# First batch of a fused attention and feed-forward kernel: numerators ahead of the inverse, kept in SBUF, and three weight transfers behind a new gate

## The chip, the cores and the metric

The kernel runs on one core of one Trainium2 chip. The metric is the device time of a whole execution in microseconds. Four executions of the kernel before took 314.83 to 316.83 us, with a median of 316.32 us.

## The reference, cut to what matters

Linear attention with cosine and sine weights, and a feed-forward layer behind it. There are 8 batches of 8 heads, 576 positions and a head size of 64. The feed-forward layer goes from 512 to 2048 and back to 512, over 8 x 576 = 4608 tokens.

```python
q_p = phi(q, cos_w, sin_w)      # relu(q) times cos and sin, side by side: 128 features
k_p = phi(k, cos_w, sin_w)
kv = einsum('bhsf,bhsd->bhfd', k_p, v)
z = sum(k_p, axis=2)
num = einsum('bhsf,bhfd->bhsd', q_p, kv)
den = einsum('bhsf,bhf->bhs', q_p, z) + 1e-06
x = num / den                   # then tokens by 512
h = x @ w_in
out = (h * sigmoid(1.702 * h)) @ w_out
```

## The kernel before

**Order.** Every engine runs its instructions in the order in which they stand in the program; the order is written out by hand, with no scheduler behind it. A prologue prepares the attention of batch 0 alone. Then a loop `i` over nine blocks of 512 tokens runs the feed-forward layer: `mm1(i, n)` for the 16 column groups `fc` of `w_in` (four matmuls and a gelu each, steps n = 0 to 15), and `mm2` for the output (64 matmuls, steps 16 to 31). Between these steps, as entries `at(n, ...)`, stands the attention of batch `i + 1`. In block 0 they start at step 6: `prep_q` (step 6, relu of q), `transpose_pe` (steps 8 to 11: TensorE transposes, then VectorE's product `qT` with cos and sin), `prep_v` (steps 8 to 12: ten VectorE products `vt`), `prep_k` (steps 13 and 14: relu of k into `kr`), `unit_kv(1)` at step 15, and `unit_den`, `unit_spread` and `unit_num` behind it.

**One batch of attention.** `unit_kv` makes the sums over positions, k times v, in two PSUM tiles, copies the sums of k into `zbuf` (L294) and the rest into `kvs` (L300). `unit_den` (L310, L314) makes the denominators; VectorE inverts them (L320), and L325 and L326 turn the inverse into `comb`. `unit_spread` (L338) spreads `comb` with 16 matmuls per batch over the 64 rows of each head, and ScalarE copies the result into SBUF as `invb` (L343). `unit_num` (L356) makes the numerators, 16 matmuls for each half `hf` of the positions, and VectorE multiplies them with `invb` into `xT` (L359), which is the input of `mm1`. A batch has four pairs of heads `j` and two halves `hf`, so eight tiles of 128 x 288.

**PSUM.** There are eight banks: four under the name `at`, two `hps`, two `yps`, each name a ring. `warmup(n)` is n matmuls whose result nobody reads.

**Transfers and their gates.** SP's queue loads q, v and k; each batch has a main part (512 positions) and a tail (64). POOL's queue loads the weights, each in four groups of 512 KB, with a change of type from float32. Two kinds of gate order them: a one-element POOL copy that reads what must have landed (L455 for `w_in`, L466 for `w_out`), and a one-element transfer on SP that reads a group of weights (L458 reads the second group of `w_in`, and batch 1's loads stand behind it; L469 reads the third group of `w_out`, and batch 2's loads stand behind it). The first four column groups of block 0 are computed outside the loop (`first`), with the contraction chunk `kc` as the outer loop.

Of the kernel before, what the change touches and what calls it, by code (L numbers as in the profile page):

```python
# [12 lines left out]
F32 = mybir.dt.float32  # L13
# [3 lines left out]
MUL = mybir.AluOpType.mult  # L17
# [11 lines left out]
def kernel(  # L29
# [9 lines left out]
    nc = tc.nc  # L39
    B, H, S, D = q.shape  # L40
    d_model = H * D
    d_ff = moe_w_in.shape[1]
    NP = H // 2
# [3 lines left out]
    HF = S // 2  # L47
    NSEG = 4
    SEG = S // NSEG
# [4 lines left out]
    two = ctx.enter_context(tc.tile_pool(name="two", bufs=2))  # L54
# [8 lines left out]
    def hps_tile():  # L63
        return ps.tile([128, TB], F32, name="hps", bufs=2)

    def yps_tile():
        return ps.tile([128, TB], F32, name="yps", bufs=2)

    def at_tile():
        return ps.tile([128, TB], F32, name="at", bufs=4)  # L70

    def warmup(n):
        for _ in range(n):
            wps = hps_tile()
            nc.tensor.matmul(wps, warm[:, 0:128], warm, start=True, stop=True)  # L75

    state = {b: {} for b in range(B)}
# [6 lines left out]
    def load_tail(t, src, b, on):  # L84
        on.dma_start(  # L85
            out=t[0:64, 2048:2560].rearrange("p (h d) -> p h d", h=H),
            in_=src[b, :, 512:576, :].rearrange("h p d -> p h d"))
# [117 lines left out]
    xT = one.tile([128, NP, B * S], BF16)  # L205
# [74 lines left out]
    def unit_kv(b):  # L280

        s = state[b]
        kv4 = [at_tile()[:, 0:2 * VW].rearrange("p (j e) -> p j e", j=2) for _ in range(2)]
        for j in range(NP):
            for c in range(5):
                for hh in range(2):
                    w = 64 * (hh ^ (j % 2))
                    nc.tensor.matmul(kv4[j // 2][w:w + 64, j % 2], kr[:, c, j, 64 * hh:64 * hh + 64],  # L288
                                     vt[:, c, 2 * j + hh, :], start=(c == 0), stop=(c == 4))
        s["kvs"], s["zs"] = [], zbuf[b % 2]  # L290
        for n, kv in enumerate(kv4):
            for hh in range(2):
                r = slice(64 * hh, 64 * hh + 64)
                nc.vector.tensor_copy(s["zs"][r, 2 * n:2 * n + 2, :, ds(12 + 16 * hh, 4)],  # L294
                                      kv[r, :, 128:130].unsqueeze(3).to_broadcast([64, 2, 2, 4]))
        for kv in kv4:
            kvs = two.tile([128, 2, 2, D], BF16, name="kvs", bufs=4)
            kv5 = kv[:, :, 0:128].rearrange("p j (cs e) -> p j cs e", cs=2)
            if b == 0:
                nc.scalar.copy(kvs, kv5)  # L300
            else:
                nc.vector.tensor_copy(kvs, kv5)
            s["kvs"] += [kvs[:, jj] for jj in range(2)]

    def unit_den(b):

        s = state[b]
        den_ps = at_tile()
        if b == 0:
            nc.tensor.matmul(den_ps[:, 0:SEG], ones[0:3, :], epsm[0:3, :], start=True, stop=False)  # L310
        for g in range(NSEG):
            for cs in range(2):
                for j in range(NP):
                    nc.tensor.matmul(den_ps[32 * j:32 * j + 32, 0:SEG], s["zs"][:, j, cs, ds(12 - 4 * g, 32)],  # L314
                                     s["qT"][:, j, cs, ds(g * SEG, SEG)],
                                     start=(b > 0 and g == 0 and cs == 0), stop=(g == NSEG - 1 and cs == 1))
        inv, pa, pb, comb = [two.tile([128, SEG], dt, name=f"den{n}", bufs=1)
                             for n, dt in enumerate((F32, F32, F32, BF16))]
        if b == 0:
            nc.vector.reciprocal(inv, den_ps[:, 0:SEG])  # L320
        else:
            nc.vector.tensor_scalar(pa, den_ps[:, 0:SEG], 1e-6, None, op0=ADD)
            nc.vector.reciprocal(inv, pa)
        for o, m in ((pa, 0), (pb, 1)):
            nc.vector.tensor_tensor(o.bitcast(I32), inv.bitcast(I32), bits[:, m:m + 1].to_broadcast([128, SEG]), op=AND)  # L325
        nc.vector.tensor_tensor(comb, pa, pb, op=SUB)  # L326
        s["comb"] = comb
        s["invb"] = {}

    def unit_spread(b, hf):  # L330
        s = state[b]
        if b == 0 and hf == 1:
            bps = [hps_tile(), hps_tile(), yps_tile(), yps_tile()]
        else:
            bps = [at_tile() for _ in range(NP)]
        for g2 in range(2):
            for j in range(NP):
                nc.tensor.matmul(bps[j][:, ds(g2 * SEG, SEG)],  # L338
                                 sel[32 * j:32 * j + 32, 2 * hf + g2].rearrange("p hh d -> p (hh d)"),
                                 s["comb"][32 * j:32 * j + 32, :], start=True, stop=True)  # L340
        for j in range(NP):
            invb = two.tile([128, HF], F32, name="invb", bufs=8)
            nc.scalar.copy(invb, bps[j][:, 0:HF])  # L343
            s["invb"][j, hf] = invb

    def unit_num(b, hf, j2s=(0, 1)):

        s = state[b]
        num_ps = {j: at_tile() for j2 in j2s for j in (2 * j2, 2 * j2 + 1)}
        for j2 in j2s:  # L350
            for cs in range(2):
                for jj in range(2):
                    j = 2 * j2 + jj
                    for hh in range(2):
                        r, w = 64 * (hh ^ jj), 64 * hh
                        nc.tensor.matmul(num_ps[j][w:w + 64, 0:HF], s["kvs"][j][r:r + 64, cs, :],  # L356
                                         s["qT"][r:r + 64, j, cs, ds(hf * HF, HF)], start=(cs == 0), stop=(cs == 1))
        for j, t in num_ps.items():
            nc.vector.tensor_tensor(xT[:, j, ds(b * S + hf * HF, HF)], t[:, 0:HF], s["invb"][j, hf], op=MUL)  # L359


    gT = {}
# [1 line left out]
    def mm1_part(hps, i, fc, kc):  # L364
        nc.tensor.matmul(hps, w_in_sb[:, kc, ds(fc * 128, 128)], xT[:, kc, ds(i * TB, TB)],  # L365
                         start=(kc == 0), stop=(kc == NP - 1))
# [69 lines left out]
    junk = const.tile([1, 16], F32)  # L436
# [23 lines left out]
    for name, src in SRC:  # L460
# [2 lines left out]
        load_part(state[1][name], src, 1, 0, H)  # L463
        if name != "kf":
            load_tail(state[1][name], src, 1, nc.sync)
    nc.gpsimd.tensor_copy(junk[:, 1:2], state[1]["vf"][0:1, 0:1])  # L466
    for g in range(4):
        nc.gpsimd.dma_start(out=w_out_sb[:, ts(g, 4), :], in_=wout_r[:, ts(g, 4), :])
    nc.sync.dma_start(out=junk[:, 9:10], in_=w_out_sb[0:1, 8, 0:2].bitcast(F32))  # L469
    load_all(2)  # L470
    warmup(14)
    unit_kv(0)
    warmup(4)
    unit_den(0)
    warmup(8)
    for hf in range(2):
        unit_spread(0, hf)
    for j2 in range(2):
        for hf in range(2):
            unit_num(0, hf, (j2,))  # L480
    first = [hps_tile(), hps_tile(), yps_tile(), yps_tile()]
    for kc in range(NP):
        for fc in range(4):
            mm1_part(first[fc], 0, fc, kc)
    for fc in range(4):
        gelu(first[fc], fc)

# [1 line left out]
    for i in range(NBLK):  # L489
        work = {n: [] for n in range(40)}  # L490
        b = i + 1
# [4 lines left out]
        if b < B:  # L496
            k0 = 6 if i == 0 else 0
            at(k0, prep_new, b)
            at(k0, prep_q, b, 0)
            at(k0, prep_q, b, 1)  # L500
            if i == 0:
                for j in range(NP):
                    at(k0 + 2 + j, transpose_pe, b, j, 0)
                    at(k0 + 2 + j, transpose_pe, b, j, 1)
            else:
                at(k0, transpose_dma, b)
                if b + 1 < B:
                    at(k0 + 1, load_all, b + 1)
            for c in range(5):
                for cs in range(2):  # L510
                    at(k0 + 2 + c, prep_v, b, c, cs)
            at(k0 + 7, prep_k, b, 0, 4)
            at(k0 + 7, prep_k_tail, b)
            at(k0 + 8, prep_k, b, 4, 8)
            if i > 0:
                for j in range(NP):
                    at(k0 + 9 + j, prep_trig, b, j)
            k1 = 15 if i == 0 else 12
            at(k1, unit_kv, b)
            at(k1 + 3, unit_den, b)  # L520
            for hf in range(2):
                at(k1 + 7 + 6 * hf, unit_spread, b, hf)
                at(k1 + 10 + 6 * hf, unit_num, b, hf)
# [49 lines left out]
```

## Time and profile before

| | |
|---|---|
| time, median of 4 (lowest to highest) | 316.32 us (314.83 to 316.83) |
| the profiled execution: time, span | 314.83 us, 312.9 us |
| PE busy | 303.3 us, 97% |
| DVE busy | 135.5 us, 43% |
| ACT busy | 135.4 us, 43% |
| POOL busy | 46.7 us, 15% |
| granted TensorE clock | 1.0 |

The span runs from the first to the last instruction of the profiled execution; 314.83 - 312.9 = 1.93 us of its time lie around the span. PE is TensorE's matmuls, PEld its weight loads, DVE VectorE, ACT ScalarE, POOL GpSimd, SP the engine that only issues transfers. In an answer of the timeline the first column is the start in us from the span's start, the second the time, and the brackets at the end tell the idle time ahead of the group and what ended it. In the chain of waits each row is a start, a duration and what held the end back in that time; the chain is followed from the last instruction backwards.

### The profile page before, as it was taken

The numbers are of one execution on the slowest core, as the hardware profiler recorded it, in microseconds if no ns is written. First come the engines' busy times: TensorE is split into PE (matmuls) and PEld (weight loads), VectorE is DVE, ScalarE is ACT, GpSimd is POOL, SyncE is SP. The second block draws the span as 40 slices with busy tenths as digits, with TensorE's granted clock in tenths as the row PEclk, the third lists the DMA queues.
The fourth block names the chain that finished last, engine by engine and source line by source line (L and its number), as shares of the span: only waits on it lengthen the run. The fifth ranks groups of instructions, "written<-read, shape, count | busy, mean of one in ns | idle before, by whom it ended". The sixth has DMA issues, their size and how long they took to land.

```text
span 312.9 us, 5644 instructions
## 1 busy us (share of the span) xinstructions
PE 303.3 (97%) x2216; PEld 139.4 (45%) x2216; DVE 135.5 (43%) x344; ACT 135.4 (43%) x260; POOL 46.7 (15%) x106
## 2 busy tenths in 40 slices
PE   8799989999999999999999999999999999999994
PEld 3444544345444544454444444544444444444443
DVE  4853863487255634654375348523952210000000
ACT  5644511463336433652365236533554346226511
POOL 7800400210220011000210120002101200011021
PEclk9999999999999999999999999999999999999999
DMA  7999999958926971596259824881500220011022
GB/s 216 272 206 312 236 197 293 236 137 257 240 67 112 330 159 67 119 326 156 67 109 289 203 68 103 279 216 52 109 18 9 60 67 0 36 67 35 2 67 67
DMA packets 60110, 45.85 MB, mean 147 GB/s; under 512 B 28916, under 2 KB 57844, under 8 KB 60084
## 3 DMA queue, kind: packets, MB, share of 16 engines
q1 hardware_dynamic: 51012, 31.60, 38.8%
q0 software_dynamic: 7328, 13.37, 19.1%
q10 hardware_dynamic: 1744, 0.52, 0.8%
q8 instruction: 17, 0.28, 0.4%
q14 instruction: 9, 0.07, 0.1%
HBM read 36.70 MB, written 9.44 MB: 147 GB/s over the span
## 4 chain that ended last, share of the span: by engine, by line
PE 85%; DMA 9%; DVE 3%; SPq 1%; POOL 0%; issue 0%; DVEq 0%
PE yps L401 38%; PE hps L365 36%; DMA vf<-in_v_dram 7%; PE at L356 3%; PE at L288 3%; DMA w_in_sb<-in_moe_w_in_dram 2%; PE hps L401 2%; DVE vt L277 1%; PE at L314 1%; PE yps L425 1%; PE at L338 1%; DVE qT L244 1%; DVE kr L217 0%; POOL w_in_sb L457 0%; SPq L80 0%; SPq L85 0%
## 5 line engine op out<-in xcount | busy, mean ns | idle before, releaser
L365 PE MATMUL hps<-xT,w_in_sb 128*128 128x512 bf16 x568 | 129.1, 378 | 0.6 <-DVE xT L359 0.4
L401 PE MATMUL yps<-w_out_sb,g 128*128 128x512 bf16 x528 | 120.5, 380 | 0.0
L370 ACT ACTIVATE g<-hps 128x512 bf16<-128x512 f32 x142 | 84.7, 597 | 55.9 <-PE hps L365 55.8
L365 PEld LDWEIGHTS <-w_in_sb 128*128 128x128 bf16 x576 | 54.8, 97 | 70.2 <-issue 10.2
L401 PEld LDWEIGHTS <-g 128*128 128x128 bf16 x560 | 51.9, 98 | 63.3 <-issue 2.9
L413 POOL DMA_DIRECT2D out_dram<-ysb x54 | 30.6, 569 | 239.4 <-ACT invb L343 129.7
L411 ACT COPY ysb<-yps 128x512 f32<-128x512 f32 x31 | 18.1, 585 | 82.7 <-PE yps L401 63.5
L359 DVE TENSOR_TENSOR xT<-at,invb 128x288 bf16<-128x288 f32 x64 | 24.7, 449 | 66.7 <-PE at L356 66.7
L343 ACT COPY invb<-at 128x288 f32<-128x288 f32 x60 | 19.7, 419 | 20.2 <-PE at L338 20.2
L430 DVE COPY ysb<-yps 128x256 f32<-128x256 f32 x1 | 0.4, 425 | 57.2 <-PE yps L425 57.2
L256 DVE TENSOR_TENSOR qT<-qTr,trig 128x1152 bf16<-128x1152 bf16 x24 | 16.6, 753 | 16.8 <-DMA qTr<-qn 14.3
L277 DVE TENSOR_SCALAR vt<-vf,cosw 128x512 bf16<-128x512 f32 (+1 forms) x40 | 18.9, 480 | 0.5 <-DMA vf<-in_v_dram 0.5
L217 DVE TENSOR_SCALAR qn<-qf 128x512 bf16<-128x512 f32 (+2 forms) x52 | 14.3, 339 | 7.0 <-DMA qf<-in_q_dram 6.8
L277 DVE TENSOR_SCALAR vt<-vf,sinw 128x512 bf16<-128x512 f32 (+1 forms) x36 | 17.3, 480 | 0.0
L75 PE MATMUL hps<-warm 128*128 128x512 bf16 x47 | 13.2, 439 | 1.2 <-DVE halfpi L121 1.2
L288 PE MATMUL at<-vt,kr 128*64 128x130 bf16 x320 | 10.9, 221 | 2.5 <-ACT kr L215 1.5
L356 PE MATMUL at<-qT,kvs 64*64 64x288 bf16 x256 | 12.2, 289 | 0.4 <-ACT invb L343 0.3
L217 DVE TENSOR_SCALAR kr<-kf 128x1024 bf16<-128x1024 f32 (+1 forms) x23 | 12.5, 591 | 0.0
L288 PEld LDWEIGHTS <-kr 128*64 128x64 bf16 x320 | 9.3, 109 | 6.2 <-issue 2.5
L356 PEld LDWEIGHTS <-kvs 64*64 64x64 bf16 x256 | 6.4, 105 | 8.0 <-issue 7.7
L75 PEld LDWEIGHTS <-warm 128*128 128x128 bf16 x47 | 4.8, 109 | 7.9 <-issue 3.2
L294 DVE CAST zbuf<-at 64x16 bf16<-64x16 f32 x32 | 5.5, 172 | 5.7 <-PE at L288 5.0
(75 smaller groups left out, 106.0 us busy)
## 6 DMA issues: line engine op xcount, KB each, us to landing
qf<-in_q_dram SPq DMA_DIRECT2D x8, 1024.0 KB, 6.1
vf<-in_v_dram SPq DMA_DIRECT2D x8, 1024.0 KB, 8.9
kf<-in_k_dram SPq DMA_DIRECT2D x7, 1024.0 KB, 11.7
out_dram<-ysb POOLq DMA_DIRECT2D x38, 128.0 KB, 2.5
out_dram<-ysb POOLq DMA_DIRECT2D x16, 256.0 KB, 2.7
w_in_sb<-in_moe_w_in_dram POOLq DMA_DIRECT2D x4, 512.0 KB, 8.5
w_out_sb<-in_moe_w_out_dram POOLq DMA_DIRECT2D x4, 512.0 KB, 9.7
kf<-in_k_dram SPq DMA_DIRECT2D x2, 512.0 KB, 11.1
```

Of the source, the lines that this page charges most:

```text
L75: nc.tensor.matmul(wps, warm[:, 0:128], warm, start=True, stop=True)
L217: on.tensor_scalar(o, i, 0.0, None, op0=MAX)
L277: on.tensor_scalar(o, i, w, None, op0=MUL)
L288: nc.tensor.matmul(kv4[j // 2][w:w + 64, j % 2], kr[:, c, j, 64 * hh:64 * hh + 64], vt[:, c, 2 * j + hh, :], start=(c == 0), stop=(c == 4))
L343: nc.scalar.copy(invb, bps[j][:, 0:HF])
L356: nc.tensor.matmul(num_ps[j][w:w + 64, 0:HF], s["kvs"][j][r:r + 64, cs, :], s["qT"][r:r + 64, j, cs, ds(hf * HF, HF)], start=(cs == 0), st ...
L359: nc.vector.tensor_tensor(xT[:, j, ds(b * S + hf * HF, HF)], t[:, 0:HF], s["invb"][j, hf], op=MUL)
L365: nc.tensor.matmul(hps, w_in_sb[:, kc, ds(fc * 128, 128)], xT[:, kc, ds(i * TB, TB)], start=(kc == 0), stop=(kc == NP - 1))
L370: nc.scalar.activation(g, hps, AF.Gelu_apprx_sigmoid)
L401: nc.tensor.matmul(yps, gT[fc][:, ds(t * 128, 128)], w_out_sb[:, fc, :], start=(fc == 0), stop=(fc == FC - 1))
L411: nc.scalar.copy(ysb, cur[t])
L413: nc.gpsimd.dma_start(out=out[row:row + (n - 1) * step + 1:step, :], in_=ysb[p0:p0 + n, :])
```

## The change

For batch 0 the numerators are made right after the denominators' matmuls, ahead of the inverse: the first half into two `hps` and two `yps` tiles, the second into four `at` tiles. ScalarE copies the eight numerator tiles into SBUF (where it copied the eight spread tiles before). Then `comb` is spread into PSUM and VectorE multiplies the spread tiles, straight from their banks, with the numerators in SBUF. The eight warmup matmuls ahead of the spread go. Half of batch 0's copies into `zbuf`, two of four, move from VectorE to ScalarE, where they stand ahead of the two `kvs` copies. The four first column groups of `mm1` run in pairs: `kc` 0 and 1 for `fc` 0 and 1, then for `fc` 2 and 3, then `kc` 2 and 3 in the same way. On POOL, the first group of `w_out` stays gated on v of batch 1, and the last three groups get a second gate, on k of batch 1. Batches 1 to 7 keep their order on every engine.

```diff
@@ unit_kv
-                nc.vector.tensor_copy(s["zs"][r, 2 * n:2 * n + 2, :, ds(12 + 16 * hh, 4)],
-                                      kv[r, :, 128:130].unsqueeze(3).to_broadcast([64, 2, 2, 4]))
+                o = s["zs"][r, 2 * n:2 * n + 2, :, ds(12 + 16 * hh, 4)]
+                i = kv[r, :, 128:130].unsqueeze(3).to_broadcast([64, 2, 2, 4])
+                if b == 0 and hh == 1:
+                    nc.scalar.copy(o, i)
+                else:
+                    nc.vector.tensor_copy(o, i)
@@ new functions: spread and num hold the matmuls of L338 and L356
+    def to_sbuf(b, hf, tiles):
+        for j in range(NP):
+            t = two.tile([128, HF], F32, name="invb", bufs=8)
+            nc.scalar.copy(t, tiles[j][:, 0:HF])
+            state[b]["sb", j, hf] = t
+
+    def product(b, hf, tiles, js=range(4)):
+        for j in js:
+            nc.vector.tensor_tensor(xT[:, j, ds(b * S + hf * HF, HF)], tiles[j][:, 0:HF], state[b]["sb", j, hf], op=MUL)
@@ the weights
-    nc.gpsimd.tensor_copy(junk[:, 1:2], state[1]["vf"][0:1, 0:1])
     for g in range(4):
+        if g < 2:
+            nc.gpsimd.tensor_copy(junk[:, 1 + g:2 + g], state[1][("vf", "kf")[g]][0:1, 0:1])
         nc.gpsimd.dma_start(out=w_out_sb[:, ts(g, 4), :], in_=wout_r[:, ts(g, 4), :])
@@ the prologue
     unit_den(0)
-    warmup(8)
     for hf in range(2):
-        unit_spread(0, hf)
-    for j2 in range(2):
+        tiles = [at_tile() for _ in range(NP)] if hf else [hps_tile(), hps_tile(), yps_tile(), yps_tile()]
+        num(0, hf, tiles)
+        to_sbuf(0, hf, tiles)
+    tiles = [[hps_tile(), hps_tile(), yps_tile(), yps_tile()], [at_tile() for _ in range(NP)]]
+    for hf in range(2):
+        spread(0, hf, tiles[hf])
+    for js in ((0, 1), (2, 3)):
         for hf in range(2):
-            unit_num(0, hf, (j2,))
+            product(0, hf, tiles[hf], js)
     first = [hps_tile(), hps_tile(), yps_tile(), yps_tile()]
-    for kc in range(NP):
-        for fc in range(4):
-            mm1_part(first[fc], 0, fc, kc)
+    for kcs, fcs in (((0, 1), (0, 1)), ((0, 1), (2, 3)), ((2, 3), (0, 1)), ((2, 3), (2, 3))):
+        for kc in kcs:
+            for fc in fcs:
+                mm1_part(first[fc], 0, fc, kc)
```

More of the change, by code (lines that the diff above doesn't have):

```diff
@@ L327, in unit_den, with spread, num @@
         s["comb"] = comb
[L328 to L335, printed above, removed]
+    def spread(b, hf, tiles):
         for g2 in range(2):
             for j in range(NP):
-                nc.tensor.matmul(bps[j][:, ds(g2 * SEG, SEG)],
+                nc.tensor.matmul(tiles[j][:, ds(g2 * SEG, SEG)],
                                  sel[32 * j:32 * j + 32, 2 * hf + g2].rearrange("p hh d -> p (hh d)"),
[L340 to L346, printed above, removed]
+                                 state[b]["comb"][32 * j:32 * j + 32, :], start=True, stop=True)
+    def num(b, hf, tiles):
         s = state[b]
-        num_ps = {j: at_tile() for j2 in j2s for j in (2 * j2, 2 * j2 + 1)}
-        for j2 in j2s:
+        for j2 in range(2):
             for cs in range(2):
@@ L355, in unit_num, with unit_spread @@
                         r, w = 64 * (hh ^ jj), 64 * hh
-                        nc.tensor.matmul(num_ps[j][w:w + 64, 0:HF], s["kvs"][j][r:r + 64, cs, :],
+                        nc.tensor.matmul(tiles[j][w:w + 64, 0:HF], s["kvs"][j][r:r + 64, cs, :],
                                          s["qT"][r:r + 64, j, cs, ds(hf * HF, HF)], start=(cs == 0), stop=(cs == 1))
-        for j, t in num_ps.items():
-            nc.vector.tensor_tensor(xT[:, j, ds(b * S + hf * HF, HF)], t[:, 0:HF], s["invb"][j, hf], op=MUL)
+    def to_sbuf(b, hf, tiles):
[6 more added lines that the diff above has]
+            nc.vector.tensor_tensor(xT[:, j, ds(b * S + hf * HF, HF)], tiles[j][:, 0:HF], state[b]["sb", j, hf], op=MUL)
+    def unit_spread(b, hf):
+        tiles = [at_tile() for _ in range(NP)]
+        spread(b, hf, tiles)
+        to_sbuf(b, hf, tiles)
+    def unit_num(b, hf):
+        tiles = [at_tile() for _ in range(NP)]
+        num(b, hf, tiles)
+        product(b, hf, tiles)
     gT = {}
```

## The prediction

> **What bounds the kernel now.** I read the page's chain by line first. It puts 85% of the span on PE, and the rest mostly on transfers:
>
> ```profile
> PE 85%; DMA 9%; DVE 3%; SPq 1%; POOL 0%; issue 0%; DVEq 0%
> ```
>
> So almost everything after the start is TensorE's own work, and the question is what sets the time at which that work can run without a break. The chain of waits in order of time answers it:
>
> ```profile
> 12.68 7.24 DMA w_in_sb<-in_moe_w_in_dram
> ...
> 21.97 11.79 DMA vf<-in_v_dram
> 33.76 0.03 issue
> 33.78 1.12 DVE vt L277 x2
> ...
> 38.60 1.58 DVE vt L277 x4
> 40.18 1.55 DVE kr L217 x3
> 41.73 0.04 issue
> 41.77 0.76 PE at L288 x20
> 42.53 1.83 PE hps L401 x8
> ```
>
> The reader is to see which lines are missing: no spread (L338), numerator (L356), product (L359) or first `mm1` of batch 0 stands between 12 and 41 us. What holds the end back there is a chain of transfers (the second group of `w_in`, SP's gate L458 behind it, then v of batch 1, landed at 33.76), and then VectorE, which prepares batch 1 from 33.78 to 41.73 without a gap. Only from 41.77, the second half of batch 1's k times v, does the chain run on PE.
>
> The timeline of PE and DVE shows the same from the other side:
>
> ```profile
> 23.65 0.60 PE L365 MATMUL hps<-xT,w_in_sb 128*128 128x512 bf16 x2
> ...
> 31.94 0.52 PE L240 MATMUL at<-ident,qn 128*128 128x128 bf16 x5
> ...
> 36.37 3.63 PE L365 MATMUL hps<-xT,w_in_sb 128*128 128x512 bf16 x16
> ...
> 40.83 1.70 PE L288 MATMUL at<-vt,kr 128*64 128x130 bf16 x40 [0.84 <-DVE kr L217]
> ```
>
> PE starts `mm1` at 23.65, is done with block 0's `mm1` at 40.0, and stands for 0.84 us until VectorE has the first half of `kr`; after the first 20 of the 40 matmuls (0.7 us) it waits again, about 0.25 us, for the second half. So PE already arrives 0.84 + 0.25 = 1.1 us before it is needed.
>
> [...] The trace agrees with the start: the first warmup matmuls follow each other by 0.43 us until about 5.9 us, later 512-column matmuls by 0.216 us; it shows no fall back, and its 0.84 us of idling at 40 us is followed by eight matmuls in 1.73 us, the full rate. [...] `vt` products on VectorE take 0.47 us, but 0.71 and 0.61 while POOL issues the four `w_out` transfers (33.93 to 36.99). [...] Here k of batch 1 (SP, issued at 29.14, landed 38.25, 9.1 us after) ran beside `w_out`.
>
> **The change part by part.**
>
> *Copies into `zbuf`.* Before, four on DVE from 15.91 to 16.77 (0.17 each by row). Now the two on DVE end near 16.6; ACT adds two. ACT has no row of this shape; its tiny operations took 0.20 to 0.28 (L145, L151), so they end near 16.95. The denominators' matmuls start at 17.43, behind four warmups that end about 17.2: nothing gained or lost. `kvs` slips from 16.35-17.22 to about 16.95-17.8; the numerators need it at 18.1. That cover is 0.3 us thin.
>
> *Numerators ahead.* They run while VectorE makes `comb` (reciprocal 1.06, two ANDs 0.53, a subtraction 0.31: 18.16 to 20.13, unchanged). Batch 1's row gives 16 matmuls in 0.69 us, so 32 take 1.4 us from 18.1; the last pair needs the bank of the denominators, which the reciprocal frees at 19.22, so they end near 19.6. They replace eight warmups (1.9 us) in the same place.
>
> *Copies to SBUF.* Still eight on ACT, 1.31 us for four: from about 18.6 to 21.1. Before they stood after `comb`; half of that time now lies beside it.
>
> *Spread and products.* The first half of the spread goes out at 20.18 (0.3 us). The second needs the `at` banks that ACT empties until 21.1, and ends near 21.4. DVE has eight products, 3.01 us before, so 0.376 each: two at 20.45, six from 21.45, the last done at 23.7 (24.69 before). `mm1` can start once the third product is done, 21.45 + 0.45 + 0.05 = 21.95, against 23.65: 1.7 us earlier. `fc` 2 and 3 wait some 0.25 us for `yps` products, so the first 16 matmuls end about 1.45 us earlier. That is what the change is worth in its own stage.
>
> *What happens to these 1.45 us.* PE's later steps up to 40.0 hold nothing that this stage feeds but gelu. The transposes of step 8 need q of batch 1 (landed 29.42, three VectorE operations, ready 30.4); PE would come to them at 31.94 - 1.45 = 30.5, just behind. So PE arrives at `unit_kv(1)` near 38.55 in place of 40.0, and there waits 40.83 - 38.55 = 2.3 us in place of 0.84. `kr` is late next, and it hangs on v's landing at 33.76 and 7.95 us of VectorE. Nothing of the change lies ahead of that landing: `w_in`'s issues, L458 and SP's order are untouched. Worth at the end: 0.
>
> *The new gate on POOL.* The copy itself is 0.17 us. What queues behind it: three `w_out` issues of 0.75 us and, much later (56.56), output stores. k's landing was 38.25 with all of `w_out` beside it, so it comes no later than that and, with one group beside it, I estimate about 36.5. The transfers of `w_out` landed 6.6, 8.8, 10.6 and 12.4 us after issues at 33.9 to 36.2: 40.5, 43.5, 46.0 and 48.6, spaced by 2.6 to 3. The bytes are the same, so I take a delay of 0 to 0.7 us for groups two to four, and 2 us as the worst (k still at 38.25, then 6.6 us for group two: 45.05). They are needed at 46.65, 50.44 and 54.62, the starts of `mm2`'s later parts: slack 3.2, 4.4 and 6.0 us. SP's L469 reads group three, so batch 2's loads slip by as much; the last tail of q landed at 49.51 + 10.2 = 59.7, and DVE reaches it at about 62.3. All of it hidden. k's earlier landing is worth nothing: at 40.10 `kr` waited for VectorE's order, not for k.
>
> *POOL against VectorE.* Ten `vt`, three `qT` and three `kr` took 7.95 us; at batch 2's pace (ten `vt` from 63.53 to 67.50, so 0.397 each) they would take 3.97 + 3 x 0.67 + 1.55 = 7.53. The excess of 0.42 lies under POOL's issues, and this is on the path. The same four issues now fall into two clumps, both still under this chain. From both sides: -0.4 (all of it gone) to +0.4 (doubled). I take -0.1.
>
> Sum: 0 for the prologue, 0 for the gate, -0.1 for POOL. Against the profiled execution's own time, 314.83 us (312.9 of span, 1.93 around it), that gives 314.7; this execution was the lowest of the four, 1.5 us under the median of 316.32, so for a median I say 316.2.
>
> **The rivals.**
>
> *A. The gain goes through.* If in executions without a profile v of batch 1 lands some 1.1 us or more earlier against PE, PE is the later one at `unit_kv(1)` and up to 1.45 us come out, with POOL's 0.4 at most 1.9: 314.4 to 314.9. For it: the four times spread by 2 us. Against it: nothing in the trace suggests that v comes earlier without a profile.
>
> *B. Slower: the array's clock falls back.* The wait at `unit_kv(1)` grows to 2.3 + 0.25 us within 3.2 us, and the warmups between denominators and spread are gone. [...] Price from the start of this trace: 0.43 in place of 0.216 per matmul over 4.7 us (1.19 to 5.9) costs 2.35 us, so 318.6. [...] no run here shows a fall back. A fall back already at 22 us would delay PE by 2.35 - 1.45 = 0.9, which the 1.1 us of slack still holds.
>
> *C. The gate starves `mm2`.* Group two would have to land after 46.65, 1.6 us past my worst case; each us beyond costs one.
>
> *D. The gate holds nothing back,* because k has landed before group one is issued. It had not: 38.25 against 34.7. Its time would be that of the forecast.
>
> **How the numbers follow.** No change: 0.75, D within it. A gain over 0.5% (1.6 us, about what a measurement of this kernel can tell from no change) needs all of A: 0.11. Slower by over 0.5%: B 0.09, C and unnamed 0.05, together 0.14. The likeliest case alone is 316.2 with -0.4 to +0.4 from POOL and about 1 us of scatter of a median. The range of 314.5 to 317.9 takes in most of A and leaves out B.
>
> **What would show it right or wrong.** Right: `mm1` starts near 22, PE's wait in front of L288 grows to about 2.3 us, its matmuls still start at 40.8 and 41.8, the chain still runs over v's landing and `vt`. Wrong: if v of batch 1 lands at another time, if L288 moves with PE, if 512-column matmuls after 42 us are spaced by 0.43 us, or if L401 shows a wait for `w_out`.

## The result, and the profile after

The changed kernel took 317.29 us (median of 43 executions; 315.08 to 319.97) against 315.69 us for the kernel before (64 executions): a ratio of 1.0038, with a 95% interval of 1.0025 to 1.0051. That is 1.2 us slower and clear of zero. The ratios here and below are those on record, with their 95% intervals; they are not quotients of the medians (here 1.0051, 1.6 us). A gain or loss in us goes by the ratio where nothing else is said. The prediction's sign, -0.1 us, was wrong, though 317.29 us lies inside its range; its base for a median, 316.32 us from four executions, was 0.6 us above the median of 64.

The profiled execution of the changed kernel took 316.54 us, with a span of 314.8 us against 312.9, so 1.9 us are to be found. The timeline of PE shows how far the prediction's picture held:

```profile
22.09 1.02 PE L376 MATMUL hps<-xT,w_in_sb 128*128 128x512 bf16 x4 [0.57 <-DVE xT L360]
...
34.85 3.63 PE L376 MATMUL hps<-xT,w_in_sb 128*128 128x512 bf16 x16
...
41.15 2.42 PE L288 MATMUL at<-vt,kr 128*64 128x130 bf16 x40 [2.68 <-DVE kr L217]
43.50 2.72 PE L412 MATMUL hps<-w_out_sb,g 128*128 128x512 bf16 x8
```

`mm1` starts at 22.09 (before: 23.65), the last `mm1` of block 0 ends near 38.5 (40.0), and PE then stands 2.68 us in front of `unit_kv(1)`. So far this is as forecast. New are the last two lines: the 40 matmuls of L288 take 2.42 us (1.70 before), and the eight 512-column matmuls behind them 2.72 us. In the kernel before these took 1.90:

```profile
42.46 1.90 PE L401 MATMUL hps<-w_out_sb,g 128*128 128x512 bf16 x8
```

The chain of waits in order of time still runs over the same landing and the same engine:

```profile
22.20 11.69 DMA vf<-in_v_dram
33.89 0.03 issue
33.92 1.12 DVE vt L277 x2
...
38.61 1.89 DVE vt L277 x4
40.50 1.14 DVE kr L217 x2
41.64 0.04 issue
41.68 1.89 PE at L288 x32
43.57 2.66 PE hps L412 x8
```

Stretches of 1 us tell why PE was slow. The columns are the stretch, its length, busy time and count of PE, PEld, DVE, ACT and POOL, then the granted TensorE clock (1.00 is full speed), the DMA share and GB/s:

```profile
40.00:41.00 1.00, 0.00 (x0) 0.00 (x0) 1.00 (x3) 0.00 (x0) 1.00 (x1) 1.00 0.37 41
41.00:42.00 1.00, 0.73 (x16) 0.57 (x18) 1.00 (x3) 0.00 (x0) 0.40 (x1) 0.90 1.14 179
42.00:43.00 1.00, 1.00 (x24) 0.96 (x22) 0.56 (x3) 0.00 (x0) 0.00 (x0) 0.50 1.20 195
43.00:44.00 1.00, 1.00 (x14) 0.55 (x10) 0.34 (x2) 0.00 (x0) 0.00 (x0) 0.50 1.21 172
44.00:45.00 1.00, 1.00 (x4) 0.36 (x3) 0.76 (x2) 0.00 (x0) 0.00 (x0) 0.50 1.07 134
45.00:46.00 1.00, 1.00 (x5) 0.41 (x4) 0.00 (x0) 0.00 (x0) 0.00 (x0) 0.90 1.23 205
46.00:47.00 1.00, 1.00 (x6) 0.29 (x3) 0.00 (x0) 0.00 (x0) 0.00 (x0) 1.00 1.17 189
```

The clock falls to half at 41.8 and comes back at 45.2: 3.4 us, since 0.10 + 3 x 0.50 + 0.10 = 1.7 us of clock are missing. In the kernel before, every stretch from 36 to 47 us had 1.00; two of them:

```profile
42.00:43.00 1.00, 1.00 (x23) 0.67 (x18) 0.56 (x4) 0.00 (x0) 0.00 (x0) 1.00 1.23 205
43.00:44.00 1.00, 1.00 (x7) 0.41 (x6) 0.72 (x2) 0.00 (x0) 0.00 (x0) 1.00 1.22 201
```

The end of `kr` on VectorE in the kernel before:

```profile
40.10 1.61 DVE L217 TENSOR_SCALAR kr<-kf 128x1024 bf16<-128x1024 f32 x3
```

And in the changed one:

```profile
40.42 1.80 DVE L217 TENSOR_SCALAR kr<-kf 128x1024 bf16<-128x1024 f32 x3
```

The 1.9 us divide so. `kr` ends at 40.42 + 1.80 = 42.22 in place of 40.10 + 1.61 = 41.71, 0.51 later: 0.13 is v's later landing, 0.38 is VectorE's chain, 8.33 us long in place of 7.95. From the end of `kr` to the first `mm1` of block 1 it is 61.42 - 42.22 = 19.20 us in place of 59.56 - 41.71 = 17.85, so 1.35 more, which I put down to the clock. 0.13 + 0.38 + 1.35 = 1.86. Behind that point both kernels take 253.3 us.

By my estimate a mean clock of 0.995 over the span is one such fall, 1.7 / 315, and 0.989 is two; 0.996 or more leaves no room for a whole one. Of the 44 listed executions of the changed kernel, 22 had at most 0.991, 19 had 0.994 or 0.995, 3 more; their medians are 317.65, 316.54 and 316.26 us. So the profiled execution is one of the milder ones.

### The profile page after: what moved, and what is told of

The parts are those of the page before. It is cut to its first block, busy times and chain, and to the rows that moved or that the text cites. A ratio compares the mean times of both kernels' runs of the same rounds, so it can differ in the third digit from the quotient of the medians.

```text
span 314.8 us, 5627 instructions
## 1 busy us (share of the span) xinstructions
PE 301.7 (96%) x2208; PEld 139.0 (44%) x2208; DVE 135.6 (43%) x342; ACT 135.6 (43%) x262; POOL 47.8 (15%) x107
## 3 DMA queue, kind: packets, MB, share of 16 engines
q1 hardware_dynamic: 51012, 31.60, 38.5%
## 4 chain that ended last, share of the span: by engine, by line
PE 85%; DMA 9%; DVE 3%; SPq 1%; POOL 0%; issue 0%; DVEq 0%
PE yps L412 37%; PE hps L376 36%; DMA vf<-in_v_dram 7%; PE at L288 3%; PE at L349 3%; PE hps L412 3%; DMA w_in_sb<-in_moe_w_in_dram 2%; DVE vt L277 1%; PE at L318 1%; PE yps L436 1%; PE at L336 1%; DVE qT L244 1%; DVE kr L217 0%; POOL w_in_sb L468 0%; SPq L80 0%; SPq L85 0%
## 5 line engine op out<-in xcount | busy, mean ns | idle before, releaser
L360 DVE TENSOR_TENSOR xT<-at,invb 128x288 bf16<-128x288 f32 x60 | 23.3, 449 | 65.2 <-PE at L349 65.2
L288 PE MATMUL at<-vt,kr 128*64 128x130 bf16 x320 | 11.6, 230 | 4.3 <-DVE kr L217 2.7
L288 PEld LDWEIGHTS <-kr 128*64 128x64 bf16 x320 | 10.0, 114 | 8.1 <-DVE kr L217 3.4
L75 PE MATMUL hps<-warm 128*128 128x512 bf16 x39 | 10.5, 425 | 1.2 <-DVE halfpi L121 1.2
L349 PE MATMUL at<-qT,kvs 64*64 64x288 bf16 x240 | 10.5, 289 | 0.2 <-DVE den L324 0.2
L412 PE MATMUL hps<-w_out_sb,g 128*128 128x512 bf16 x32 | 8.6, 410 | 0.0
```

The source lines that it names most:

```text
L349: nc.tensor.matmul(tiles[j][w:w + 64, 0:HF], s["kvs"][j][r:r + 64, cs, :], s["qT"][r:r + 64, j, cs, ds(hf * HF, HF)], start=(cs == 0), sto ...
L412: nc.tensor.matmul(yps, gT[fc][:, ds(t * 128, 128)], w_out_sb[:, fc, :], start=(fc == 0), stop=(fc == FC - 1))
```

## The experiments

Three readings had to be told apart. **T**: the clock falls because PE waits too long ahead of `unit_kv(1)`. **R**: the new gate makes `kr` late, and the clock is a by-product. **W**: the fall comes from the eight warmups that are gone. Each run was timed against the kernel before, over 59, 59 and 43 executions of it in the three groups; PE waits and landings are those of each kernel's one profile. `warmup(n)` serves as filler here: n matmuls whose result nobody reads.

**Group one: the gate and the wait.** The prologue without the new gate:

```diff
-        if g < 2:
+        if g < 1:
             nc.gpsimd.tensor_copy(junk[:, 1 + g:2 + g], state[1][("vf", "kf")[g]][0:1, 0:1])
```

> The changed kernel with w_out's four groups all gated on v of batch 1, as before the change; the new prologue stays. Theory T (TensorE's clock falls to half because its wait ahead of batch 1's k times v has grown from 0.84 to 2.7 us; the new gate adds only some 0.3 to 0.5 us of it, since POOL's issues now stand beside VectorE's last vt and kr): the wait shrinks to about 2.3 us, kr ends near 41.7 as before the change, the clock falls in some executions only, so 0 to 1.3 us above the kernel before. Rival R (the new gate makes kr late, and that alone is the loss; the clock is a by-product that costs nothing): as the kernel before, within 0.2 us, whatever the clock does.

Ratio 1.0041 (1.0023 to 1.0060), 317.8 us: all of the loss is there without the gate. R falls. PE waited 3.15 us (v landed at 34.54, later than in the profiles so far), the clock was at half from 41.95 to 45.36, and all 22 executions had a mean clock of 0.995 or less. My figure for T, a fall in some executions only, was too mild.

The gate alone, in the kernel before:

```diff
-    nc.gpsimd.tensor_copy(junk[:, 1:2], state[1]["vf"][0:1, 0:1])
     for g in range(4):
+        if g < 2:
+            nc.gpsimd.tensor_copy(junk[:, 1 + g:2 + g], state[1][("vf", "kf")[g]][0:1, 0:1])
```

> The kernel before with the k gate alone on w_out's last three groups; the old prologue stays. T: PE arrives at 40.0 as before the change, waits 1.2 to 1.3 us, the granted clock stays 1.0, kr ends 0.3 to 0.5 us later: 0.3 to 0.5 us above the kernel before. R: the whole loss, 1.2 us or more.

Ratio 1.0008 (0.9986 to 1.0030). PE waited 0.95 us (forecast 1.2 to 1.3) and kept its clock. VectorE's chain from v's landing to the end of `kr` took 8.15 us, against 7.95 before and 7.96 in e1_no_k_gate: the gate's price is 0.2 to 0.4 us of VectorE, too little for these timings to confirm.

The changed kernel with eight unread matmuls in PE's wait, with the gate and without:

```diff
+            if i == 0:
+                at(k1, warmup, 8)
             at(k1, unit_kv, b)
```

> The changed kernel with eight warmup matmuls (1.7 us on PE, result unread) ahead of batch 1's k times v, in PE's wait. T: clock 1.0 throughout, the 512-column matmuls at 43 us spaced by 0.216 us; only the late kr is left, 0.3 to 0.5 us above the kernel before and about 0.9 below the changed one. R: as the changed kernel, 1.2 us above the kernel before, or more for the added matmuls.

> The changed kernel without the k gate and with the eight warmup matmuls in PE's wait. T: both costs gone, as the kernel before within 0.2 us: the new prologue's 1.5 us stay lost in the wait. R: the same, as the gate is gone. A third case, in which the new prologue costs something of its own, would leave it above the kernel before.

Ratios 0.9995 (0.9973 to 1.0018) and 0.9985 (0.9969 to 1.0001). Added work on PE took the loss away. The filler stands on PE alone and behind v's landing, so it also decides a rival that none of the three letters covers, that the new prologue only makes v of batch 1 land later: with the same prologue, and v as late as 35.58 us in its profile, e4_fill8_no_gate has a median of 315.56 us against 317.80 for e1_no_k_gate, 22 executions each. Nor did the eight warmups of the prologue have to come back, which speaks against W. The timeline of PE in e3_fill8:

```profile
38.66 2.32 PE L75 MATMUL hps<-warm 128*128 128x512 bf16 x8
41.76 1.88 PE L288 MATMUL at<-vt,kr 128*64 128x130 bf16 x40 [0.78 <-DVE kr L217]
43.58 1.90 PE L412 MATMUL hps<-w_out_sb,g 128*128 128x512 bf16 x7
```

PE starts L288 even later than the changed kernel (41.76, as v landed later), yet the matmuls behind run at full rate (1.90). No stretch from 7 to 60 us shows a lower clock. In the profile of e4_fill8_no_gate there is a fall at another place, in batch 0's prologue:

```profile
22.00:23.00 1.00, 0.73 (x2) 0.26 (x2) 1.00 (x4) 0.00 (x0) 0.00 (x0) 0.56 1.22 202
23.00:24.00 1.00, 0.78 (x3) 0.38 (x3) 1.00 (x3) 0.00 (x0) 0.00 (x0) 0.50 1.25 209
```

It starts at 22.1. Six of that kernel's 22 executions had a mean clock of 0.992 to 0.995, and their median was 315.56 us, the same as that of the other 16. So a fall up there, if that is what those six had, cost nothing here: PE still waited 0.75 us for `kr` in that profile.

**Group two: how long a wait, and from where.** Three unread matmuls in place of eight (`at(k1, warmup, 3)`):

> The changed kernel with three warmup matmuls in PE's wait ahead of batch 1's k times v, where e3_fill8 has eight. T: some 0.65 us of the wait is filled, plus what the first of them waits for its bank, and the rest, about 2 us, stays: the fall of the clock at 41 us comes in fewer executions than in the changed kernel, so the median lies between 0 and 1.2 us above the kernel before. If the fall needs a window without any matmul, three are enough and it is as e3_fill8 (0 to 0.3 us above the kernel before).

Ratio 1.0037 (1.0015 to 1.0058): as bad as the changed kernel, so T's "fewer" did not show. PE waited 1.72 us behind them, and its clock fell at 43.2. In the 3.4 us ahead of that PE had been busy for about 1.5 us, so this fall came without a stretch of that length free of work. Its profile, with a mean clock of 0.989, also shows a fall at 22.7.

The wait without the new prologue: the kernel before, with the first half of batch 1's `kr` written four times, so that PE waits for it longer.

```diff
-            at(k0 + 7, prep_k, b, 0, 4)
+            for _ in range(4 if i == 0 else 1):
+                at(k0 + 7, prep_k, b, 0, 4)
```

> The kernel before with batch 1's first half of kr written four times by VectorE in place of once (0.67 us each), so that PE waits about 2.0 us longer there, with the old prologue and all its warmups. T: 2.0 us of delay and on top of it the clock's fall at 42 us, 1 to 2.5 us more: 3.0 to 4.5 us above the kernel before. Rival W (the fall comes from the eight warmups that the new prologue leaves out, not from the wait): 2.0 us above, clock as before.

Ratio 1.0090 (1.0058 to 1.0122), 2.8 us, from six executions; the medians are 3.7 us apart. The interval holds W's 2.0 us as well and lies in good part under T's 3.0 to 4.5, so the time alone does not decide. The stretches do:

```profile
42.00:43.00 1.00, 0.00 (x0) 0.00 (x0) 0.97 (x2) 0.00 (x0) 0.00 (x0) 0.88 1.23 204
43.00:44.00 1.00, 0.61 (x12) 0.61 (x14) 1.00 (x3) 0.00 (x0) 0.00 (x0) 0.50 1.25 208
44.00:45.00 1.00, 1.00 (x24) 1.00 (x22) 0.45 (x3) 0.00 (x0) 0.00 (x0) 0.50 1.22 204
```

With the old prologue and all warmups, a wait of 3.20 us brings the clock down at 42.8, and all six executions have a mean clock of 0.994 or 0.995. The wait alone is enough for the fall: W is not needed. About 0.8 us of the 2.8 are left for the clock above the planned delay of 2.0, a size that these six executions don't show firmly; some executions of the kernel before lose the clock too (15 of 59 in this group had 0.995 or less), which makes the difference smaller.

The warmups put back into the changed kernel (`warmup(8)` behind `unit_den(0)`):

> The changed kernel with the eight warmup matmuls put back behind the denominators' matmuls. They delay the numerators by 1.7 us, so that part or all of the prologue's gain goes, and PE's wait at batch 1's k times v shrinks by up to 1.4 us. T: the time follows that wait: with about 1.3 to 1.8 us of it left the fall at 41 us is rarer, 0 to 0.9 us above the kernel before. W: the same or less; what tells them apart is the trace: by W no fall anywhere, by T a fall at 41 us wherever the wait is still over 2 us.

Ratio 1.0015 (0.9996 to 1.0035). `mm1` starts at 24.11, the prologue's gain is gone, PE waits 0.73 us, and there is no fall near 41 us; that fits T, and it would fit W too. But its profile has a fall from 25.2 to 28.6, with the warmups in place, which W does not allow. In 16 of 22 executions the mean clock was 0.995 or less, so T's "rarer" holds for the place near 41 us in this profile and not for falls as such.

**Making use of the gain.** If `kr` is what PE waits for, it should be ready earlier. Its VectorE queue has `qT` products in front that `unit_kv(1)` does not read. In the changed kernel without the gate I moved the last two behind `kr`, and the second half of `kr` to ScalarE:

```diff
-                    at(k0 + 2 + j, transpose_pe, b, j, 1)
+                    if j < 2:
+                        at(k0 + 2 + j, transpose_pe, b, j, 1)
...
-            at(k0 + 8, prep_k, b, 4, 8)
+            if i > 0:
+                at(k0 + 8, prep_k, b, 4, 8)
+            else:
+                at(15, prep_k, b, 4, 8, AC)
+            if i == 0:
+                for j in (2, 3):
+                    at(k0 + 8, transpose_pe, b, j, 1)
```

> The changed kernel without the k gate, with batch 1's second half of kr on ScalarE (free from 39.1, when its last gelu of block 0 is done) and the last two of batch 1's qT products behind kr on VectorE. T: kr is ready near 40.0 in place of 41.7, PE's wait is about 1.2 us, the clock stays up, and the time falls by 1.0 to 1.8 us below the kernel before: the prologue's gain then reaches the end. If the bound is elsewhere (w_out's first group, which landed at 40.5 before), 0 to 0.5 us below.

Ratio 0.9984 (0.9963 to 1.0006), which is not clear of no change: not T's forecast, and within the second branch. v landed at 35.1 in its profile, and PE still waited 1.98 us, then 0.57 us for `w_out`'s first group; 12 of 22 executions had a clock of 0.995 or less, though the profiled one kept it at 1.00 through both waits. Group three filled that wait with five unread matmuls (`at(k1, warmup, 5)`), and tried the `qT` move by itself in the kernel before:

> e8_defer_act with five warmup matmuls in PE's remaining wait ahead of batch 1's k times v. T: kr stays ready 0.6 to 1.5 us earlier than in the kernel before, and no execution loses the clock at 41 us any more: 0.8 to 1.6 us below the kernel before. If kr's earlier end is worth nothing (w_out's first group or v of batch 1 decides), it is as e4_fill8_no_gate, 0 to 0.5 us below.

> The kernel before with one move on VectorE alone: the last two of batch 1's qT products behind kr. Old prologue, no new gate. T: PE still arrives at 40.0, kr is ready near 40.4 in place of 41.7, so PE hardly waits there: no fall of the clock at 41 us, and 0.8 to 1.5 us below the kernel before, though batch 0's prologue is not a bit shorter. If PE's arrival were what counts, no difference.

e9_defer_act_fill5: 0.9987 (0.9971 to 1.0003), a miss. PE reached `unit_kv(1)` early, and L288 started at 40.42, bound by v's landing at 34.55. e10_before_defer: **0.9969 (0.9955 to 0.9984)**, 314.69 us against 315.49, a gain of 1.0 us, as T had forecast, and faster than both kernels. Its timeline of PE:

```profile
36.59 3.63 PE L365 MATMUL hps<-xT,w_in_sb 128*128 128x512 bf16 x16
40.14 1.55 PE L288 MATMUL at<-vt,kr 128*64 128x130 bf16 x40
41.63 1.90 PE L401 MATMUL hps<-w_out_sb,g 128*128 128x512 bf16 x7
```

No bracket stands behind L288: PE comes out of `mm1` into `unit_kv(1)` without a wait, and `mm2` starts at 41.63 in place of 42.46. The old prologue is untouched. The clock seems not to be the larger part of this gain: among executions with a mean clock of 0.996 or more the medians are 314.43 us (18 executions) and 315.35 (31).

Not settled: v of batch 1 landed at 33.76 to 34.14 in the four profiles with the old prologue and at 33.89 to 35.6 in the eight with the new one. One profile of each cannot say whether the prologue moves it; no instruction that loads it was changed. In e4_fill8_no_gate and e7_warm8_back the delay begins with the group of `w_in` ahead of v, 8.64 and 8.87 us in flight against 7.24 in the kernel before. It may be why e9 gained less than e10. Where the second fall lies in executions of the changed kernel with a mean clock of 0.989 is not known either; in e5_fill3, the only profile with that mean, it lies in the prologue.

## Why the prediction was right or wrong

- *The bound.* Right: chain and timeline of the kernel before named v's landing and VectorE's chain, and the changed kernel's chain runs over the same two. e10, which shortens nothing but that chain and gains 1.0 us, confirms it.
- *The prologue's own gain.* Right in size: the last product over at 23.86 (forecast 23.7), `mm1` at 22.09 (21.95), PE at `unit_kv(1)` near 38.5 (38.55). Right that none of it reaches the end.
- *"`kr` is late next ... Worth at the end: 0."* This step failed. It priced the longer wait at nothing because PE was not the bound. Here the wait grew from 0.84 to 2.68 us and took the clock away from the work behind it, 1.35 us in the profiled execution; eight matmuls that fill it bring the loss back to nothing (0.9995).
- *Rival B* named this mechanism and this place and got 0.09. What failed in it is how much idling it took the fall to need: no trace had shown that, and I held the forecast wait to be too short. PE's wait was 2.68 us, and in the 3.4 us ahead of the fall (38.38 to 41.79) PE was busy for 0.62 us; e5_fill3 fell with about 1.5 us of work in 3.4, and the wait of 0.78 us in e3_fill8, which leaves about 2.4 us of work in 40.0 to 43.4, did not bring a fall. The price of 2.35 us was too high for one fall here: it lasts 3.4 us, not 4.7, so 1.7 us at most, and the wait for the second half of `kr` probably hides a part.
- *The kernel before as a witness.* I took its wait of 0.84 us, which the clock survived, as evidence that a wait there is harmless. It was one profile. A mean clock of 0.995 or less in 23 of 59 executions says that the kernel before is not always at full clock either; their median is 316.91 us, that of the other 36 is 315.50. Where those falls lie no profile shows.
- *POOL against VectorE.* The term was -0.1, from -0.4 to +0.4; it measured +0.38 in the changed kernel, the upper end. The three late issues (38.23 to 41.40) lay beside the last `vt` and `kr`: two of those `vt` took 0.67 and 0.60 us in place of 0.47, `kr` 1.80 in place of 1.61, and one POOL issue 1.53 in place of 0.74. In e1_no_k_gate, which leaves out the second gate, the last `vt` took 0.47 and `kr` 1.61. So the two were slower beside each other; no run here tells how.
- *The gate.* Right that it neither starves `mm2` nor speeds anything up: k landed at 38.1 (38.25), not at the 36.5 that I had estimated, and no wait for `w_out` shows.

## What to carry to other kernels

When an edit only makes an engine arrive earlier at a wait that something else ends, price the longer wait as well: on TensorE it cost 1.2 us here, where the edit saved nothing at the end. Either shorten what ends the wait, beginning with work that stands in its queue and isn't needed for it (e10), or keep TensorE busy through it (e3_fill8 and e4_fill8_no_gate, ratios 0.9995 and 0.9985). The mean granted clock of each execution is the cheapest sign, as a single profile can miss a fall (e8_defer_act: 0.999 in the profile, 0.995 or less in 12 of 22 executions); it does not say where the fall lies, and one in a stage that TensorE leaves early anyway may cost nothing (e4_fill8_no_gate: a median of 315.56 us with a mean clock of at most 0.995 and above it).

## What the runs showed of the hardware that I had not expected

The falls were all equally long. The changed kernel's clock was at half from 41.79 to 45.21, 3.41 us. The stretches up to 97 us show six more, near 41 to 43 us and in the prologue: one each in e1_no_k_gate, e4_fill8_no_gate, e6_before_late_kr and e7_warm8_back, and two in e5_fill3, from 22.7 to 26.1 and from 43.2 to 46.6. In each of the six 1.71 us of clock are missing, so 3.4 us at half. The clock also fell behind the last matmul: at 313.22 in the kernel before, whose last matmul was over at 308.5, and at 314.86 in the changed one, 310.3. Why a kernel loses the clock ahead of it in some executions only, no run here tells.

The clock fell although TensorE had done some work. In the 3.4 us ahead of its fall, as long a stretch as the fall itself, PE was busy for 0.34 us (e1_no_k_gate), 0.62 (changed kernel), 0.85 (e6_before_late_kr) and about 1.5 (e5_fill3, near 43 us). Busy time alone doesn't tell a fall from none: e8_defer_act had 1.47 us of work from 37.50 to 40.91, and its clock stayed. Its work there was 512-column matmuls alone; in e5_fill3 it was a few of these and then smaller ones of L288. In the prologue, where many matmuls are small too, the clock fell with about 2.0 us of work in the 3.4 us ahead (e5_fill3, at 22.7), 2.1 (e4_fill8_no_gate, at 22.1) and 2.4 (e7_warm8_back, at 25.2). What decides between these cases stays open.
